# Split activations in slots at 256, 320 and 384 modulo 512 bytes, in place of one offset for all

## The chip, the core and the metric

The kernel runs on one core of a Trainium2 chip. The metric is the device time of one execution in microseconds (us).

## What is computed

Three stages follow each other, all on float32 numbers. `relu2` attention without a softmax comes first, then an MLP with a leaky relu, then an MLP with a squared relu:

```
B, S, D = 2, 3008, 256;  d_qk = 64;  d_ff = 2048
scores = (z @ z.T) / S;  attn = maximum(scores, 0) ** 2
x = u * (attn @ v)                                  # 6016 rows of 256
h = x @ w1_in;   x = maximum(0.01 * h, h) @ w1_out
h = x @ w2_in;   y = (s * maximum(h, 0) ** 2 + b) @ w2_out
```

## The kernel before

**Precision.** A float32 matrix product is made of three products in the type `float32r`. Every operand is split into a rounded part `hi` and the rest `lo`, and the kernel adds hi·hi, hi·lo and lo·hi in PSUM. Activations that are made on the way are split by `split_parts`, which hands out a pair of tiles `hi` and `lo`. Each is 128 partitions by 2 by 512 float32 numbers, so 4096 bytes in each partition. The pool `parts` keeps three slots for `hi` and three for `lo`, used in turn.

**Tiles.** There are 12 tiles of tokens. Ten have 512 columns and two have 448. A matmul's moving operand is a row of 512 or 448 columns, 2048 or 1792 bytes in a partition. Its weights are 128 columns, 512 bytes.

**Attention** (lines L351 and L425). It has 12 steps for each tile, 144 in all. A step makes the scores of two blocks of keys (six matmuls L351, weights `zk`, moving `zq`), then adds the values of an earlier step (24 matmuls L425, weights `stat_v`, moving `hi` and `lo`). These matmuls use 64 rows, and two of them, one for each half of the rows, run at once. So a step has 3 pairs of scores and 12 pairs of values. The square of the scores is split by `att_parts`.

**MLPs** (lines L500 and L519). The loop `for m, pr, q in quads` has 96 passes: 2 MLPs, 6 pairs of tiles, 8 blocks of d_ff. `product` (L500) makes the first layer from seven Strassen products of three matmuls each, with weights `stat_i` and moving operand `top`. `queue_second` (L519) makes the second layer with weights `stat_o` and moving operand `hi` and `lo` of the pass before. Each tile of a pass has 12 such matmuls. They are taken from a queue, eight after each third of the first-layer products. So in a pass 21 matmuls of L500 alternate with three runs of eight of L519, and a tile's twelve lie in two of these runs.

**Places in SBUF.** The pools lie one behind the other from the left (from low addresses), and `edge`, `z` and `c` from the right end. Worked out from the declarations and read from the built program, every SBUF operand of these matmuls begins, modulo 512 bytes in its partition, at 256 when it lies left, and at 448 when it lies right:

| operand | read by | before | after |
|---|---|---|---|
| weights `stat_v`, `stat_i`, `stat_o` | L425, L500, L519 | 256 | 256 |
| `hi`, `lo` | L425, L519 | 256 in all three slots | 256, 320, 384 by slot |
| `zk` (weights) and `zq` | L351 | 448 | 320 |
| `top` of B11 and T2, every second pair | L500 | 448 | 320 |
| all other `top` | L500 | 256 | 256 |

Parts within a tile lie multiples of 512 bytes apart, so the offset holds for each of them. B11 and T2 take their `top` from `cpool` on the right for every second pair of tiles. `tpool` on the left serves the others. There are four such pairs of 512 columns and two of 448 in the 12 pairs of both MLPs, with 8 passes each.

**Order.** [...] The program writes out each engine's list, and semaphores hold an instruction until its operands are there. `keep_busy` (L614) puts matmuls on a tile of zeros, which takes a `hi` slot, ahead of the first scores and again at step 2.

Of the kernel before, what the change touches and what calls it, by code (L numbers as in the profile page):

```python
# [10 lines left out]
F32 = mybir.dt.float32  # L11
F32R = mybir.dt.float32r
# [4 lines left out]
P = 128  # L17
# [3 lines left out]
QT = 512  # L21
# [7 lines left out]
def relu2_attention__then__leaky_mlp__then__relu2_mlp_kernel(  # L29
# [52 lines left out]
    parts = ctx.enter_context(tc.tile_pool(name="parts", bufs=3))  # L82
# [234 lines left out]
    def take(n):  # L317
        for _ in range(min(n, len(queue))):
            queue.popleft()()

    def split_parts(a, n):
        hi = parts.tile([P, 2, QT], F32R, tag="hi", name="hi")
        lo = parts.tile([P, 2, QT], F32R, tag="lo", name="lo")
        return [(y[:, :, :n]) for y in (hi, lo)]


# [16 lines left out]
    def scores(t, p):  # L343

        n = tiles[t][2]
        f = ps_f.tile([P, 2, QT], F32, tag="f", name="f")
        for i, (wh, xh) in enumerate(((0, 0), (1, 0), (0, 1))):
            for j in range(2):
                kb, rows = 2 * p + j, slice(j * DZ, (j + 1) * DZ)
                lhsT = zk[tiles[t][0], kb // 4][rows, wh, kb % 4 // 2, :]  # L350
                nc.tensor.matmul(f[:, j, :n], lhsT=lhsT, rhs=zq[t][rows, xh, :n], start=i == 0, stop=i == 2)  # L351
        return f[:, :, :n]
# [10 lines left out]
    def first_parts(f):  # L363

        a = work.tile([P, 2, QT], F32, tag="a", name="a")
        hi, lo = split_parts(a, QT)
        for j in range(2):
            nc.scalar.activation(out=a[:, j], in_=f[:, j], func=AF.Relu, scale=scale)
            nc.scalar.activation(out=a[:, j], in_=a[:, j], func=AF.Square)
            nc.vector.tensor_copy(out=hi[:, j], in_=a[:, j])  # L370
            nc.vector.tensor_sub(out=lo[:, j], in0=a[:, j], in1=hi[:, j].bitcast(F32))
        return hi, lo

    def att_parts(t, p, a):
        hi, lo = split_parts(a, tiles[t][2])
        (nc.scalar.copy if p % 2 and (t or p > 1) else nc.vector.tensor_copy)(out=hi, in_=a)  # L376
        nc.vector.tensor_sub(out=lo, in0=a, in1=hi.bitcast(F32))  # L377
        return hi, lo
# [195 lines left out]
    with tc.manual_schedule():  # L574
# [3 lines left out]
        raw_pool = lctx.enter_context(tc.tile_pool(name="raw", bufs=3))  # L578
        single = lctx.enter_context(tc.tile_pool(name="single", bufs=1))
        edge = ctx.enter_context(tc.tile_pool(name="edge", bufs=1, side="right"))  # L580
        edge.tile([P, 8], F32, tag="edge", name="edge")
        zpool = rctx.enter_context(tc.tile_pool(name="z", bufs=2, side="right"))
        ps_f = fctx.enter_context(tc.tile_pool(name="ps_f", bufs=2, space=bass.MemoryType.PSUM))
        tpool = cpool = ps_x = None
# [20 lines left out]
            if i:  # L605
                load_v(0, g, into=v_early.get(g))

        zeros = parts.tile([P, 2, QT], F32R, tag="hi", name="zeros")
        nc.vector.memset(zeros[:, 0].bitcast(F32), 0.0)  # L609
        idle = ps_a.tile([P, QT], F32, tag="acc", name="idle")  # L610

# [100 lines left out]
        for step in range(n_att):  # L712
# [6 lines left out]
            f = scores(t, p)  # L719
# [41 lines left out]
        def spread(ti):  # L761

            if not before:
                return
            m, pr, q, cs = before
            c = cs[ti]
            hi, lo = split_parts(c, tiles[pr[0]][2])
            (nc.scalar.copy if m == 1 else nc.vector.tensor_copy)(out=hi, in_=c)  # L768
            nc.vector.tensor_sub(out=lo, in0=c, in1=hi.bitcast(F32))  # L769
            queue_second(m, pr, q, ti, hi, lo)  # L770
# [9 lines left out]
        for m, pr, q in quads:  # L780
            n = tiles[pr[0]][2]
            k = pair_of.index((m, pr))
# [102 lines left out]
```

## Time and profile before

| | |
|---|---|
| median of two runs | 1460.42 us (1460.34 to 1460.51) |
| the profiled execution | 1460.41 us |
| its span, first to last instruction | 1458.6 us |
| outside the span | 1.8 us |
| PE (matmuls) busy | 1453.2 us, 100% |
| PEld (weight loads, beside PE) busy | 1211.4 us, 83% |
| DVE busy | 1113.1 us, 76% |
| ACT busy | 920.3 us, 63% |
| POOL busy | 91.6 us, 6% |

The profile is one execution. PE's busy time is from a matmul's start to its modelled end, and matmuls overlap, so a busy PE says only that some matmul is always under way. What a matmul costs is the time from its start to the start of the next. The attention runs until 474 us, the MLPs to the end.

### The profile page before, as it was taken

To read this page: it belongs to the slowest core of one execution; us is meant where nothing else is said; L and a number is where in the kernel's file an instruction comes from. 1 tells how busy PE (TensorE), PEld (TensorE's weight loads), DVE (VectorE), ACT (ScalarE), POOL (GpSimd) and SP (SyncE) were. 2 spreads that over 40 slices of the span, in tenths; PEclk is the share of its full clock that TensorE was granted. 3 is DMA by queue.
4 is the path that set the end of the run, shared out by engine and by line. 5 is a ranking of instruction groups with operands and counts; after the bars stand their busy time and mean duration, and the time that the engine had idled before them with its cause. 6 is when DMAs were issued, how large, how long until landed. Compare 5 with 4: busy or idle time off the path is not lost.

```text
span 1458.6 us, 20850 instructions
## 1 busy us (share of the span) xinstructions
PE 1453.2 (100%) x8584; PEld 1211.4 (83%) x8584; DVE 1113.1 (76%) x1461; ACT 920.3 (63%) x1143; POOL 91.6 (6%) x71
## 2 busy tenths in 40 slices
PE   9999999999999999999999999999999999999998
PEld 7888888888888788888889888888888888988887
DVE  7999978999986566666657666667878777787866
ACT  8888888988888455454555555554545455555544
POOL 1221200221214000000000000000000000000000
PEclk9999999999999999999999999999999999999999
DMA  5244333544545301000000103330010101010000
GB/s 177 80 161 160 142 121 112 163 149 163 181 168 200 143 0 58 1 26 29 23 36 15 41 0 124 143 139 28 19 40 1 55 1 58 1 54 1 22 8 29
DMA packets 40319, 112.03 MB, mean 77 GB/s; under 512 B 4128, under 2 KB 16544, under 8 KB 38176
## 3 DMA queue, kind: packets, MB, share of 16 engines
q1 hardware_dynamic: 39792, 110.31, 21.6%
q8 instruction: 67, 1.10, 0.3%
q10 hardware_dynamic: 368, 0.39, 0.1%
q14 instruction: 28, 0.23, 0.0%
q0 software_dynamic: 64, 0.00, 0.0%
HBM read 69.14 MB, written 41.55 MB: 76 GB/s over the span
## 4 chain that ended last, share of the span: by engine, by line
PE 100%; DVE 0%; ACT 0%; issue 0%
PE acc L519 35%; PE x L500 31%; PE acc L425 26%; PE f L351 7%; PE idle L614 0%; PE acc L446 0%; ACT y_half L548 0%; DVE x_sb L543 0%; DVE zeros L609 0%; PE f L566 0%; DVE ones L594 0%
## 5 line engine op out<-in xcount | busy, mean ns | idle before, releaser
L500 PE MATMUL x<-top,stat_i 128*128 128x512 f32 (+1 forms) x2016 | 499.1, 386 | 0.0
L519 PE MATMUL acc<-hi,stat_o 128*128 128x512 f32 (+1 forms) x1536 | 483.4, 386 | 0.0
L500 PEld LDWEIGHTS x<-top,stat_i 128*128 128x128 f32 x2016 | 377.6, 188 | 74.5 <-issue 1.2
L425 PE MATMUL acc<-hi,stat_v 64*128 64x512 f32 (+1 forms) x2256 | 366.2, 384 | 0.0
L519 PEld LDWEIGHTS acc<-hi,stat_o 128*128 128x128 f32 x1536 | 288.3, 188 | 55.5 <-issue 0.2
L519 PE MATMUL acc<-lo,stat_o 128*128 128x512 f32 (+1 forms) x768 | 296.2, 386 | 0.0
L769 DVE TENSOR_TENSOR lo<-c,hi 128x1024 fp32r<-128x1024 f32 (+1 forms) x192 | 230.6, 1201 | 38.3 <-ACT hi L768 35.1
L792 ACT COPY a<-x 128x512 f32<-128x512 f32 (+1 forms) x96 | 55.5, 578 | 319.7 <-PE x L500 319.2
L425 PEld LDWEIGHTS acc<-hi,stat_v 64*128 64x128 f32 x2256 | 211.6, 184 | 43.6 <-issue 1.1
L377 DVE TENSOR_TENSOR lo<-a,hi 128x1024 fp32r<-128x1024 f32 (+1 forms) x143 | 197.4, 1380 | 27.7 <-ACT hi L376 24.0
L425 PE MATMUL acc<-lo,stat_v 64*128 64x512 f32 (+1 forms) x1104 | 214.2, 385 | 0.0
L519 PEld LDWEIGHTS acc<-lo,stat_o 128*128 128x128 f32 x768 | 144.1, 188 | 27.4
L357 ACT ACTIVATE a<-f 128x1024 f32<-128x1024 f32 (+1 forms) x143 | 143.5, 1003 | 17.1 <-PE f L351 11.4
L359 ACT ACTIVATE a<-a 128x1024 f32<-128x1024 f32 (+1 forms) x143 | 149.4, 1045 | 4.2
L795 DVE TENSOR_TENSOR a<-x,a 128x512 f32<-128x512 f32 (+1 forms) x96 | 65.3, 680 | 84.5 <-PE x L500 83.5
L829 DVE TENSOR_TENSOR c<-x,a 128x512 f32<-128x512 f32 (+1 forms) x96 | 65.3, 680 | 77.0 <-PE x L500 77.0
L425 PEld LDWEIGHTS acc<-lo,stat_v 64*128 64x128 f32 x1104 | 103.4, 184 | 22.1 <-issue 0.7
L351 PE MATMUL f<-zq,zk 64*128 64x512 f32 (+1 forms) x864 | 121.7, 387 | 0.0
L759 ACT ACTIVATE c<-c 128x1024 f32<-128x1024 f32 (+1 forms) x96 | 100.2, 1044 | 3.0
L768 ACT CAST hi<-c 128x1024 fp32r<-128x1024 f32 (+1 forms) x96 | 98.7, 1028 | 1.5
L351 PEld LDWEIGHTS f<-zq,zk 64*128 64x128 f32 x864 | 81.3, 185 | 16.8 <-ACT zq L300 0.7
L818 DVE TENSOR_TENSOR c<-x,a 128x512 f32<-128x512 f32 (+1 forms) x96 | 65.1, 678 | 38.1 <-PE x L500 37.5
(84 smaller groups left out, 1072.2 us busy)
## 6 DMA issues: line engine op xcount, KB each, us to landing
in_d<-stage_i SPq DMA_DIRECT2D x16, 896.0 KB, 5.9
stat_i<-in_d SPq DMA_DIRECT2D x16, 896.0 KB, 4.6
x_in<-x_d SPq DMA_DIRECT2D x20, 512.0 KB, 4.2
raw_w<-in_w_in_dram SPq DMA_DIRECT2D x16, 512.0 KB, 4.0
raw_w<-in_w_out_dram SPq DMA_DIRECT2D x16, 512.0 KB, 3.9
out_d<-stage_o SPq DMA_DIRECT2D x8, 1024.0 KB, 6.6
stat_o<-out_d SPq DMA_DIRECT2D x8, 1024.0 KB, 6.5
u_sb<-in_uT_dram SPq DMA_DIRECT2D x10, 512.0 KB, 5.6
```

Of the source, the lines that this page charges most:

```text
L351: nc.tensor.matmul(f[:, j, :n], lhsT=lhsT, rhs=zq[t][rows, xh, :n], start=i == 0, stop=i == 2)
L357: nc.scalar.activation(out=a, in_=f, func=AF.Relu, scale=scale)
L359: nc.scalar.activation(out=a, in_=a, func=AF.Square)
L377: nc.vector.tensor_sub(out=lo, in0=a, in1=hi.bitcast(F32))
L425: nc.tensor.matmul(acc[:, :n], lhsT=w[rows, wh, o:o + P], rhs=x[rows, blk % 2, :n], start=blk == 0 and i == 0, stop=bool(closing and last),)
L500: nc.tensor.matmul(x[:, :n], lhsT=w[:, wh, left, :], rhs=r[:, xh, :n], start=first and i == 0, stop=i == 2, skip_group_check=not first,)
L519: nc.tensor.matmul(acc[dh][:, :n], lhsT=w[:, q % 2, wh, o:o + P], rhs=x[:, f, :n], start=q == 0 and f == 0 and i == 0, stop=last,)
L759: nc.scalar.activation(out=c, in_=c, func=AF.Square)
L768: (nc.scalar.copy if m == 1 else nc.vector.tensor_copy)(out=hi, in_=c)
L769: nc.vector.tensor_sub(out=lo, in0=c, in1=hi.bitcast(F32))
L795: nc.vector.tensor_tensor(out=u2, in0=x2, in1=s1, op=ALU.add)
L829: nc.vector.tensor_tensor(out=c21, in0=x2, in1=s1, op=ALU.add)
```

## The change

The three slots become three pairs of tiles with names of their own (`hi0`, `lo0`, `hi1`, ...), in the order hi0, lo0, a gap of 64 bytes, hi1, lo1, a gap of 64 bytes, hi2, lo2, and a gap of 384 bytes. The split with the number k takes slot k modulo 3. What follows in the left pools begins at 256 again. `edge` grows from 32 to 160 bytes, so that what lies on the right moves from 448 to 320. The tile of zeros lies in `hi0`.

```diff
+    GAPS = (0, 64, 64, 384)
+    for k, gap in enumerate(GAPS):
+        if gap:
+            parts.tile([P, gap // 4], F32, tag=f"gap{k}", name="gap", bufs=1)
+        if k < 3:
+            for name in ("hi", "lo"):
+                parts.tile([P, 2, QT], F32R, tag=f"{name}{k}", name=name, bufs=1)
+    places_of = iter(range(1 << 20))
+
     def split_parts(a, n):
-        hi = parts.tile([P, 2, QT], F32R, tag="hi", name="hi")
-        lo = parts.tile([P, 2, QT], F32R, tag="lo", name="lo")
+        k = next(places_of) % 3
+        hi = parts.tile([P, 2, QT], F32R, tag=f"hi{k}", name="hi", bufs=1)
+        lo = parts.tile([P, 2, QT], F32R, tag=f"lo{k}", name="lo", bufs=1)
         return [(y[:, :, :n]) for y in (hi, lo)]
...
-        edge.tile([P, 8], F32, tag="edge", name="edge")
+        edge.tile([P, 40], F32, tag="edge", name="edge")
...
-        zeros = parts.tile([P, 2, QT], F32R, tag="hi", name="zeros")
+        zeros = parts.tile([P, 2, QT], F32R, tag="hi0", name="zeros", bufs=1)
```

On every engine the instructions stand in the same order as before, ten lines further down in the file. What moves is one wait of DVE at the start of the program. Before, DVE's list from the first split on reads so (`hi` and `lo` are the split parts, `a` the squared scores, `stat_v` and `zk` parts of the weights):

```order
L370 CAST hi<-a 128x512 [waits Activation_49]
L371 TENSOR_TENSOR lo<-a,hi 128x512 [waits DVE_49]
L370 CAST hi<-a 128x512 [waits Activation_49]
L371 TENSOR_TENSOR lo<-a,hi 128x512 [waits DVE_49]
L637 CAST stat_v<-raw_v 128x256 [waits DMAHW2_49]
L638 TENSOR_TENSOR stat_v<-raw_v,stat_v 128x256 [waits DVE_49]
L376 CAST hi<-a 128x1024 [waits Activation_49]
L377 TENSOR_TENSOR lo<-a,hi 128x1024 [waits DVE_49]
L116 TENSOR_TENSOR stat_v<-raw_v,stat_v 128x768 [waits DMAHW6_49,Activation_49]
L292 CAST zk<-zr_early 128x256 [waits DMAHW7_49,DMAHW0_49]
L293 TENSOR_TENSOR zk<-zr_early,zk 128x256 [waits DVE_49]
L376 CAST hi<-a 128x1024 [waits PE_49,Activation_49]
```

And now, the same stretch of DVE's list:

```order
L380 CAST hi<-a 128x512 [waits PE_49,Activation_49]
L381 TENSOR_TENSOR lo<-a,hi 128x512 [waits DVE_49]
L380 CAST hi<-a 128x512 [waits Activation_49]
L381 TENSOR_TENSOR lo<-a,hi 128x512 [waits DVE_49]
L647 CAST stat_v<-raw_v 128x256 [waits DMAHW2_49]
L648 TENSOR_TENSOR stat_v<-raw_v,stat_v 128x256 [waits DVE_49]
L386 CAST hi<-a 128x1024 [waits Activation_49]
L387 TENSOR_TENSOR lo<-a,hi 128x1024 [waits DVE_49]
L116 TENSOR_TENSOR stat_v<-raw_v,stat_v 128x768 [waits DMAHW6_49,Activation_49]
L292 CAST zk<-zr_early 128x256 [waits DMAHW7_49,DMAHW0_49]
L293 TENSOR_TENSOR zk<-zr_early,zk 128x256 [waits DVE_49]
L386 CAST hi<-a 128x1024 [waits Activation_49]
```

The wait for PE has gone from the third split to the first. In both programs it is a wait for the same point of PE's list, the 24th matmul, which is the last of the five idle ones of step 2 that read the tile of zeros. The first split now overwrites that tile, where before the third did.

## Rows read from the trace of the kernel before

**Rows 1.** The page's first, second and fourth part: PE, its granted clock, the chain.

```profile
PE 1453.2 (100%) x8584; PEld 1211.4 (83%) x8584; DVE 1113.1 (76%) x1461; ACT 920.3 (63%) x1143; POOL 91.6 (6%) x71
...
PEclk9999999999999999999999999999999999999999
...
PE 100%; DVE 0%; ACT 0%; issue 0%
```

**Rows 2.** Groups by line and shape: count | busy us, mean ns | idle before.

```profile
L500 PE MATMUL x<-top,stat_i 128*128 128x512 f32 x1680 | 422.6, 390 | 0.0
L519 PE MATMUL acc<-hi,stat_o 128*128 128x512 f32 x1280 | 407.8, 389 | 0.0
...
L425 PE MATMUL acc<-hi,stat_v 64*128 64x512 f32 x1880 | 308.9, 387 | 0.0
...
L519 PE MATMUL acc<-lo,stat_o 128*128 128x512 f32 x640 | 249.3, 389 | 0.0
...
L425 PE MATMUL acc<-lo,stat_v 64*128 64x512 f32 x920 | 180.4, 389 | 0.0
...
L519 PE MATMUL acc<-hi,stat_o 128*128 128x448 f32 x256 | 76.3, 367 | 0.0
...
L519 PE MATMUL acc<-lo,stat_o 128*128 128x448 f32 x128 | 47.0, 367 | 0.0
```

**Rows 3.** PE in order of time, MLP, 512 columns: start us, us, matmuls.

```profile
580.24 1.56 PE L500 MATMUL x<-top,stat_i 128*128 128x512 f32 x6
...
581.64 0.85 PE L500 MATMUL x<-top,stat_i 128*128 128x512 f32 x3
...
583.25 0.39 PE L519 MATMUL acc<-lo,stat_o 128*128 128x512 f32 x1
...
584.15 1.52 PE L500 MATMUL x<-top,stat_i 128*128 128x512 f32 x6
...
590.50 2.02 PE L500 MATMUL x<-top,stat_i 128*128 128x512 f32 x8
```

**Rows 4.** PE in order of time, MLP, 448 columns.

```profile
756.02 1.40 PE L500 MATMUL x<-top,stat_i 128*128 128x448 f32 x6
...
761.81 1.37 PE L500 MATMUL x<-top,stat_i 128*128 128x448 f32 x6
...
763.02 0.78 PE L500 MATMUL x<-top,stat_i 128*128 128x448 f32 x3
```

**Rows 5.** PE in order of time, one attention step, 512 columns.

```profile
101.03 0.85 PE L351 MATMUL f<-zq,zk 64*128 64x512 f32 x6
101.72 0.39 PE L425 MATMUL acc<-hi,stat_v 64*128 64x512 f32 x2
...
103.33 0.39 PE L425 MATMUL acc<-lo,stat_v 64*128 64x512 f32 x2
...
104.46 0.85 PE L351 MATMUL f<-zq,zk 64*128 64x512 f32 x6
```

**Rows 6.** PE in order of time, one attention step, 448 columns.

```profile
230.27 0.77 PE L351 MATMUL f<-zq,zk 64*128 64x448 f32 x6
...
233.31 0.77 PE L351 MATMUL f<-zq,zk 64*128 64x448 f32 x6
```

**Rows 7.** DVE's subtractions by line: duration ns min/median/max.

```profile
L377 DVE TENSOR_TENSOR lo<-a,hi x143: 1084/1225/2360, 11.9 to 478.6; 128x1024 fp32r<-128x1024 f32 x119, 128x896 fp32r<-128x896 f32 x24
...
L769 DVE TENSOR_TENSOR lo<-c,hi x192: 1081/1224/1227, 491.2 to 1448.4; 128x1024 fp32r<-128x1024 f32 x160, 128x896 fp32r<-128x896 f32 x32
```

**Rows 8.** All engines in order of time, the first splits.

```profile
7.33 1.42 PE L614 MATMUL idle<-zeros 128*128 128x512 f32 x5
...
8.04 0.43 DVE L370 CAST hi<-a 128x512 fp32r<-128x512 f32 x1 [1.05 <-ACT a L369]
...
9.65 0.69 DVE L371 TENSOR_TENSOR lo<-a,hi 128x512 fp32r<-128x512 f32 x1
...
10.40 0.19 PEld L425 LDWEIGHTS acc<-lo,stat_v 64*128 64x128 f32 x2 [0.26 <-DVE lo L371]
```

## The prediction

> **What bounds the kernel now.** I read the page's totals and its chain first. PE is busy for 1453.2 us of the span of 1458.6 us, and the chain of work that ended last is PE's for 100% of its length [rows 1]. [...] The groups by line then show no idle time before PE's matmuls [rows 2]. PE thus paces the kernel, and what counts is the time from the start of one matmul to the start of the next. That is read from the view in order of time.
>
> There the same instruction does not always take the same time, and the offsets are what differs. In the MLP from 584.15 to 590.50 us, 28 matmuls of 512 columns, both operands at 256, take 6.35 us, or 226.8 ns each [rows 3]. The six from 580.24 to 581.64 us are B11 and T2 of a pair whose `top` lies at 448, with weights at 256. They take 1.40 us, 233.3 ns each [rows 3]. Engines, waits and shapes are the same. After them the moving offset is back at 256, but the next seven matmuls, to 583.25 us, still take 1.61 us, 230.0 ns each, before 226.8 returns [rows 3]. I call that settling: 0.023 us after each such group. With 448 columns the order is reversed. 28 matmuls at equal offsets, from 756.02 to 761.81 us, take 5.79 us, 206.8 ns each, and the six at 448 over 256, from 761.81 to 763.02 us, take 201.7 ns [rows 4]. So the distance between the offset of the moving operand and that of the weights costs up to 6.5 ns in a matmul, in either direction.
>
> In the attention the scores have both operands at 448 and the values both at 256, so that the distance changes where one follows the other. The three pairs of scores take 0.69 us, 230 ns each, and the seven pairs of values behind them 1.61 us, again 230 ns. The last five are at 226 ns [rows 5]. A step takes 3.43 us, where 15 pairs at 226.8 ns would be 3.40 us, so 0.03 us of it is settling. A step of 448 columns takes 3.04 us, 202.7 ns a pair, and doesn't settle at 206.8 at all [rows 6].
>
> **The change part by part.** It removes and adds no instruction. It gives two thirds of all splits a distance of 64 or 128 bytes from the weights, moves scores and some `top` from 448 to 320, and moves one wait of DVE.
>
> *How many.* Matmuls of 512 columns on `hi` and `lo`: 1280 and 640 in the MLPs, and 1880 and 920 in the attention, which run two at once, so 1400 pairs [rows 2]. That is 3320 steps of PE, a third of them, 1107, in each slot. Of 448 columns the MLPs have 256 and 128, so 128 in each slot [rows 2]. The attention's of 448 are left as they are, since they don't keep to either level now.
>
> *The price of 64 and of 128* is not in the trace. The measured distances are 0 and 192, at 226.8 and 233.3 ns. The bounds are one such step of 6.5 ns to either side of 226.8, since the 448-column rows show that a distance can also gain. I take each at the row that it is nearest to: 64 as 0, 128 as 192.
>
> - Slot 2, at 128: 1107 by 6.5 ns is +7.2 us. Its 448-column matmuls save 128 by 5.1 ns, -0.7 us.
> - Slot 1, at 64: 0, with bounds of -7.2 and +7.2 us.
> - Settling in the MLPs: a pass has two tiles with two runs each. The 80 passes of 512 columns have 320 runs, of which 107 lie in slot 2. At 0.023 us, +2.5 us.
> - `top` at 320 in place of 448, so 64 and taken as 0: four pairs by 8 passes by 6 matmuls are 192 by -6.5 ns, -1.2 us. Two pairs of 448 columns are 96 by +5.1 ns, +0.5 us. 32 settlings fall away, -0.7 us. Together -1.4 us.
> - Scores at 320: in slots 0 and 1 they now stand within 64 of the values, so the settling of 0.03 us falls away in two thirds of the 120 steps of 512 columns, -2.4 us. If it stays, 0.
> - The wait: the first split (8.04 us) now waits for the five idle matmuls, which end at 7.33 + 1.42 = 8.75 us [rows 8], so it starts 0.7 us later. Behind it on DVE stand its subtraction, the second split and its subtraction, almost back to back, the last of which ends at 10.34 us. PE waits for that one already, 0.26 us at 10.40 us [rows 8]. So nothing hides it there: +0.7 us, at least 0 if the lists make it up. The third split loses the wait, which was over long before.
> - DVE and ACT: no cost. The subtraction with operands at 448 and 256 (L769) has a median of 1224 ns, and that with both at 256 (L377) one of 1225 ns [rows 7]. Their durations don't follow the offset, and PE doesn't wait for them but at the start.
>
> The sum is 7.2 - 0.7 + 0 + 2.5 - 1.4 - 2.4 + 0.7 = **+5.9 us**. The profiled execution took 1460.41 us, the median is 1460.42, so they need no correction: **1466.3 us**.
>
> [...]
>
> **The rivals.**
>
> A, the forecast: nearest rows, 1466 us.
>
> B, both new distances are a step cheaper. For it speaks that distance gains 5.1 ns at 448 columns [rows 4]. Against it: in the long run no stretch of 512 columns stands under 226 ns. 2213 matmuls by -6.5 ns are -14.4 us. `top` gains 13 ns on 192, -2.5 us, and 0.7 us of settling. All 120 steps lose their settling, -3.6 us. With the wait, -20.5 us: 1440 us.
>
> C, slower: both distances cost what 192 does, and three offsets in turn keep PE from ever settling. Its place is the runs of L519 and the whole attention step. 2213 by 6.5 ns is +14.4 us, 213 runs by 0.023 us +4.9 us, and five more pairs in each step at 230 in place of 226.8 ns +1.9 us. 256 matmuls of 448 columns save 1.3 us. With the wait, +20.6 us: 1481 us. It decides from the point at which 64 costs what 192 does. For it: one change of distance is enough to unsettle seven matmuls [rows 3]. Against it: 64 is nearer to 0.
>
> D, the change doesn't do what it says: something else than distance makes the 6.5 ns (that `top` lies in another pool, say), and only the wait is left, 1461 us. Against it: a few microseconds later the same line runs at 226.8 ns from the left pool, in both widths with opposite signs [rows 3, 4]. [...]
>
> **How the numbers follow.** A 0.40, B 0.25, C 0.20, D 0.15. A's own range, by slot 1 and the settling in the attention, is 1457 to 1474 us. For 8 in 10 I go from 1444 us, which leaves out the part of B that reaches its full price (0.12), to 1478 us, which leaves out the end of C (0.08). About 2% of the time, 29 us, is what a measurement of this kernel can tell from no change. Under 1431 us needs more than B's full price, over 1490 us a distance that costs some 13 ns on all 2213 matmuls. I give each 0.03 and leave 0.94 for no change.
>
> **What would show it.** The view in order of time, by slot: runs of L519 on slot 0 near 227 ns, on slot 1 the same, on slot 2 near 233, and B11 and T2 of every second pair at 227. In the attention, steps of slots 0 and 1 at 3.40 us. At the start, the first split at about 8.75 us and PE's wait of 10.40 us about 0.7 us later. If slot 1 stands near 220 or 233 ns, the price of 64 is wrong and B or C is right. If all slots stand at 226.8, D is. What would upset the whole sum is that a matmul's time depends on the offsets of its neighbours in more ways than one distance, so that no slot has a price of its own.

## The result, and the profile after

The changed kernel took 1474.37 us (1473.31 and 1475.43 in two runs) against 1460.42 us before. The ratio is 1.0093, with a 95% interval of 1.0073 to 1.0114. It is thus about 0.9% slower: the interval lies clear of 1, but inside the 2% that counts as no change here. The profiled execution took 1473.31 us with a span of 1471.5 us, 12.9 us longer than the 1458.6 us of before. Lines of the changed kernel stand ten lower in its file from the first edit on: L351, L425, L500 and L519 are now L361, L435, L510 and L529.

The page of the changed kernel (busy times, granted clock, the chain by engine) answers to [rows 1]:

```profile
PE 1465.4 (100%) x8584; PEld 1213.0 (82%) x8584; DVE 1112.8 (76%) x1461; ACT 921.3 (63%) x1143; POOL 91.6 (6%) x71
...
PEclk9999999999999999999999999999999999999999
...
PE 99%; DVE 0%; DMA 0%; ACT 0%; issue 0%; DVEq 0%
```

PE has the same 8584 instructions at the same granted clock (0.999 and 1.000 on average), and grew from 1453.2 to 1465.4 us of busy time. DVE and ACT moved by 1 us at most. So the loss lies in PE's own pace and in no other engine.

The groups by line and shape (count | busy us, mean ns | idle before) answer to [rows 2]:

```profile
L510 PE MATMUL x<-top,stat_i 128*128 128x512 f32 x1680 | 425.4, 392 | 0.0
L529 PE MATMUL acc<-hi,stat_o 128*128 128x512 f32 x1280 | 412.6, 393 | 0.0
L435 PE MATMUL acc<-hi,stat_v 64*128 64x512 f32 x1880 | 311.8, 391 | 0.0
```

Their mean durations rose by 2 to 4 ns, without idle time. Since matmuls overlap (those of 512 columns in the table below last 387 to 393 ns on average and start 227 to 234 ns apart), I summed the time from each start to the next over the whole trace of either kernel, by line and width. Two matmuls on 64 rows that start together (3 ns apart at the median in both traces) count once, and the very last matmul, which has no next, is left out:

| line of before, columns | matmuls | before, us | after, us | difference |
|---|---|---|---|---|
| L351 scores, 512 | 360 | 84.3 | 84.0 | -0.3 |
| L425 values, with L446, 512 | 1410 | 322.7 | 327.5 | +4.8 |
| L500 `top` products, 512 | 1680 | 384.3 | 387.0 | +2.7 |
| L519 split products, 512 | 1920 | 435.8 | 443.2 | +7.4 |
| L500, 448 | 336 | 68.7 | 68.2 | -0.5 |
| L519, 448 | 384 | 79.0 | 77.8 | -1.2 |

The rest of PE's work is unchanged to 0.1 us, and the sum is +12.9 us, the difference of the spans.

PE in order of time, MLP, 512 columns, answers to [rows 3]:

```profile
600.08 1.53 PE L510 MATMUL x<-top,stat_i 128*128 128x512 f32 x6
601.45 0.63 PE L529 MATMUL acc<-hi,stat_o 128*128 128x512 f32 x2
...
603.30 1.53 PE L510 MATMUL x<-top,stat_i 128*128 128x512 f32 x6
...
611.88 0.62 PE L529 MATMUL acc<-hi,stat_o 128*128 128x512 f32 x2
...
615.06 0.39 PE L529 MATMUL acc<-lo,stat_o 128*128 128x512 f32 x1
...
622.66 0.62 PE L529 MATMUL acc<-hi,stat_o 128*128 128x512 f32 x2
...
624.52 1.54 PE L510 MATMUL x<-top,stat_i 128*128 128x512 f32 x6
```

The allocation tells which slot each piece reads. From 601.45 to 603.30 us eight split products read slot 1 (320) and take 1.85 us, 231 ns each. The six `top` products ahead of them, at 256, take 1.37 us, 228 ns each, though both their operands lie at 256. From 611.88 to 615.06 us everything is at 256, and 14 products take 3.18 us, 227 ns each. From 622.66 to 624.52 us eight products read slot 2 (384) and take 1.86 us, 232.5 ns each. Over the trace the means of L519 are 228.6 ns in slot 0, 231.7 in slot 1 and 232.5 in slot 2, against 227.1 before.

The scores of five attention steps in a row answer to [rows 5]:

```profile
102.51 0.86 PE L361 MATMUL f<-zq,zk 64*128 64x512 f32 x6
...
105.94 0.85 PE L361 MATMUL f<-zq,zk 64*128 64x512 f32 x6
...
109.43 0.85 PE L361 MATMUL f<-zq,zk 64*128 64x512 f32 x6
...
112.91 0.86 PE L361 MATMUL f<-zq,zk 64*128 64x512 f32 x6
...
116.35 0.85 PE L361 MATMUL f<-zq,zk 64*128 64x512 f32 x6
```

From one start to the next is a step. In slots 0, 1, 2 and 0 again they take 3.43, 3.49, 3.48 and 3.44 us, where the steps took 3.43 us before [rows 5].

The start, all engines in order of time, answers to [rows 8]:

```profile
7.23 1.41 PE L624 MATMUL idle<-zeros 128*128 128x512 f32 x5
...
8.75 0.43 DVE L380 CAST hi<-a 128x512 fp32r<-128x512 f32 x1 [1.64 <-PE idle L624]
...
11.02 0.18 PEld L435 LDWEIGHTS acc<-lo,stat_v 64*128 64x128 f32 x2 [0.53 <-DVE lo L381]
...
12.99 0.86 PE L361 MATMUL f<-zq,zk 64*128 64x512 f32 x6
```

In the trace of before, the scores that now start at 12.99 us started here:

```profile
12.33 0.85 PE L351 MATMUL f<-zq,zk 64*128 64x512 f32 x6
```

The first cast waits for the idle products, as foreseen, and PE is 0.66 us later behind it.

### The profile page after: what moved, and what is told of

It is laid out like the page before. It is cut to its first block, busy times and chain, and to the rows that moved or that the text cites. A ratio compares the mean times of both kernels' runs of the same rounds, so it can differ in the third digit from the quotient of the medians.

```text
span 1471.5 us, 20850 instructions
## 1 busy us (share of the span) xinstructions
PE 1465.4 (100%) x8584; PEld 1213.0 (82%) x8584; DVE 1112.8 (76%) x1461; ACT 921.3 (63%) x1143; POOL 91.6 (6%) x71
## 4 chain that ended last, share of the span: by engine, by line
PE 99%; DVE 0%; DMA 0%; ACT 0%; issue 0%; DVEq 0%
PE acc L529 35%; PE x L510 31%; PE acc L435 26%; PE f L361 7%; DMA zr<-in_zT_dram 0%; PE acc L456 0%; DVE lo L381 0%; PE idle L624 0%; DVE zq L301 0%; DVE zk L634 0%; DVE hi L380 0%; ACT y_half L558 0%; DVE x_sb L553 0%; PE f L576 0%; DVE zk L632 0%
## 5 line engine op out<-in xcount | busy, mean ns | idle before, releaser
L510 PE MATMUL x<-top,stat_i 128*128 128x512 f32 (+1 forms) x2016 | 501.5, 388 | 0.0
L529 PE MATMUL acc<-hi,stat_o 128*128 128x512 f32 (+1 forms) x1536 | 487.5, 388 | 0.0
L510 PEld LDWEIGHTS x<-top,stat_i 128*128 128x128 f32 x2016 | 377.7, 188 | 77.6 <-issue 1.2
L435 PE MATMUL acc<-hi,stat_v 64*128 64x512 f32 (+1 forms) x2256 | 369.0, 386 | 0.0
L529 PEld LDWEIGHTS acc<-hi,stat_o 128*128 128x128 f32 x1536 | 288.5, 188 | 58.4 <-issue 0.2
L529 PE MATMUL acc<-lo,stat_o 128*128 128x512 f32 (+1 forms) x768 | 298.1, 388 | 0.0
L435 PEld LDWEIGHTS acc<-hi,stat_v 64*128 64x128 f32 x2256 | 212.3, 185 | 45.1 <-issue 1.1
L435 PE MATMUL acc<-lo,stat_v 64*128 64x512 f32 (+1 forms) x1104 | 215.7, 388 | 0.3 <-DVE lo L381 0.2
L529 PEld LDWEIGHTS acc<-lo,stat_o 128*128 128x128 f32 x768 | 144.3, 188 | 29.4
L435 PEld LDWEIGHTS acc<-lo,stat_v 64*128 64x128 f32 x1104 | 103.8, 185 | 22.9 <-DVE lo L381 1.1
L361 PE MATMUL f<-zq,zk 64*128 64x512 f32 (+1 forms) x864 | 121.1, 385 | 0.4 <-DVE zq L301 0.4
L361 PEld LDWEIGHTS f<-zq,zk 64*128 64x128 f32 x864 | 81.1, 184 | 17.8 <-DVE zq L301 0.8
```

The costliest lines, as they stand in the source:

```text
L435: nc.tensor.matmul(acc[:, :n], lhsT=w[rows, wh, o:o + P], rhs=x[rows, blk % 2, :n], start=blk == 0 and i == 0, stop=bool(closing and last),)
L510: nc.tensor.matmul(x[:, :n], lhsT=w[:, wh, left, :], rhs=r[:, xh, :n], start=first and i == 0, stop=i == 2, skip_group_check=not first,)
L529: nc.tensor.matmul(acc[dh][:, :n], lhsT=w[:, q % 2, wh, o:o + P], rhs=x[:, f, :n], start=q == 0 and f == 0 and i == 0, stop=last,)
```

## The experiments

**The halves of the change.** The first kernel moves only the right-hand pools, the second only the slots (the change without its edit of `edge`, which stays at 8). The edit of the first:

```diff
-        edge.tile([P, 8], F32, tag="edge", name="edge")
+        edge.tile([P, 40], F32, tag="edge", name="edge")
```

> The kernel before with one half of the change: the right-hand pools at 320 modulo 512, the split activations' slots all at 256 as they were. Distance theory (each 64-byte distance between the two operands of a matmul has a price of its own: from the changed kernel's intervals about 231 ns at 64, 232.5 at 128, 233.3 at 192 against 226.7 at 0 for 512 columns, 201 to 203 against 206.7 for 448): the scores and the early top products go from distance 192 to 64, 360 x -0.9 ns, 192 x -2.7 ns, together about -1 us: 1459.5 us (1457 to 1461). Change theory (a constant distance is free, only going from one distance to another costs some 24 ns over six matmuls): just as many changes as before, 1460.4. Right-pool theory (the loss comes from the right-hand pools): the whole +13.9, 1474.

> The other half alone: slots at 256, 320 and 384, the right-hand pools back at 448. Distance theory: the split products of the MLP and the values as in the changed kernel, that is +7.4 - 1.2 + 4.8, and the share of the third line's intervals that settles after a change, about +3: 1474 us (1471 to 1477). Change theory: the same size, since the slots alternate just as often. Right-pool theory: only the wait at the start, 1461.

Measured: the right-hand pools alone 1461.21 us, ratio 1.0004 (0.9995 to 1.0013); the slots alone 1472.74 us, 1.0083 (1.0069 to 1.0096). The loss lies with the slots. One thing in my first expectation was careless: scores have queries and keys both in right-hand pools, so their own distance was 0 before and after, and the -0.9 ns on them had no ground.

**One distance throughout.** The next kernels give every moving operand, split halves, `top` and queries, the same distance from its weights, which all stay at 256. At distance 0 the edge alone does it:

```diff
-        edge.tile([P, 8], F32, tag="edge", name="edge")
+        edge.tile([P, 56], F32, tag="edge", name="edge")
```

For distance d a gap of d bytes goes ahead of the slots and of the queries, and the edge is sized to match; here d = 64:

```diff
+        if not zq:
+            zpool.tile([P, 16], F32, tag="zgap", name="zgap", bufs=1)
         m = zpool.tile([P, 2, QT], F32R, tag="zq", name="zq", bufs=2)
...
+    parts.tile([P, 16], F32, tag="gap", name="gap", bufs=1)
...
-        edge.tile([P, 8], F32, tag="edge", name="edge")
+        edge.tile([P, 40], F32, tag="edge", name="edge")
```

> From the kernel before: every moving operand (split halves, early top products, scores) and its weights at the same place, 256 modulo 512; nothing ever changes its distance. Distance theory: scores 360 x about -5 ns, values 1410 x -1.9, early top 192 x -7, their neighbours 1488 x -1.4, against 168 products of 448 columns at +5: together -7, 1453.5 us (1450 to 1458). Change theory: the same -7. A theory by which offsets do nothing: 1460.4.

> From the kernel before: every moving operand 64 bytes above its weights modulo 512, all through; nothing ever changes its distance. This tells two theories apart. Distance theory: 5,370 products of 512 columns at +4.3 ns and 1,074 of 448 columns at -5.7 ns against the run with distance 0, +17: about 1470 us (1465 to 1476). Change theory: as the run with distance 0, 1453.5 (1450 to 1458).

> Every moving operand 128 bytes above its weights modulo 512, all through. Graded theory (the level rises with the distance): slot 2 of the changed kernel took 0.8 ns more than slot 1, 5,370 x 0.8 over the run with distance 64: 1467.5 us (1465 to 1471). Theory of one step (any distance but 0 costs the same once it is constant): 1463.1 (1461 to 1465).

> Every moving operand 192 bytes above its weights, all through. Graded theory: the early top products of the kernel before (448 over 256) took 233.3 to 233.7 ns; 5,370 x 6.7 over distance 0, less 1,074 products of 448 columns x 2: 1489 us (1480 to 1490). Theory of one step: 1463.1 (1461 to 1465), and then 233.3 is the cost of the change, not of the distance.

> Every moving operand 256 bytes from its weights modulo 512. The level theory holds by now for 0, 64, 128 and 192 (1454.8, 1463.1, 1485.0 and 1487.8 us); open is its shape, and so where one should put operands that can't lie together. Mirror theory (only the shorter way round 512 counts): the top of the curve, 1489 us (1486 to 1494). Theory of 256 (the distance counts modulo 256): as distance 0, 1454.8 (1453 to 1457). One-way theory (rises all the way to 512): 1490 (1487 to 1496).

> Distance 320. Mirror theory: as 192, 1488 us (1485 to 1491). Theory of 256: as 64, 1463 (1461 to 1466). One-way theory: above 192, 1492 (1489 to 1500).

> Distance 384. Mirror theory: as 128, 1485 us (1482 to 1488). Theory of 256: as 128 as well, 1485. One-way theory: 1495 (1490 to 1510).

> Distance 448, the moving operand 64 bytes below its weights. Mirror theory: as 64, 1463 us (1461 to 1466). Theory of 256: as 192, 1488 (1485 to 1491). One-way theory: the dearest of all, 1500 (1490 to 1520).

Measured, with the mean from start to start of L519's products in the MLP:

| distance | us | ratio to before (95%) | 512 columns, ns | 448 columns, ns |
|---|---|---|---|---|
| 0 | 1454.80 | 0.9964 (0.9951 to 0.9978) | 226.9 | 202.6 |
| 64 | 1463.08 | 1.0017 (1.0008 to 1.0025) | 229.4 | 200.1 |
| 128 | 1485.01 | 1.0169 (1.0155 to 1.0183) | 232.4 | 203.6 |
| 192 | 1487.84 | 1.0184 (1.0170 to 1.0198) | 233.4 | 202.3 |
| 256 | 1454.37 | 0.9961 (0.9946 to 0.9976) | 226.9 | 202.5 |
| 320 | 1462.10 | 1.0013 (1.0004 to 1.0022) | 229.0 | 200.1 |
| 384 | 1484.47 | 1.0161 (1.0146 to 1.0176) | 232.4 | 203.5 |
| 448 | 1487.02 | 1.0182 (1.0165 to 1.0199) | 233.4 | 202.3 |

PE in order of time in five of these kernels. Each pair of rows holds the same 14 products of 512 columns, six of `top` and eight of L519 (here L519 or L523), and the second row starts the next ones. Distance 0:

```profile
613.02 1.52 PE L500 MATMUL x<-top,stat_i 128*128 128x512 f32 x6
...
616.19 1.52 PE L500 MATMUL x<-top,stat_i 128*128 128x512 f32 x6
```

Distance 64:

```profile
605.08 1.54 PE L504 MATMUL x<-top,stat_i 128*128 128x512 f32 x6
...
608.29 1.53 PE L504 MATMUL x<-top,stat_i 128*128 128x512 f32 x6
```

Distance 128:

```profile
613.41 1.56 PE L504 MATMUL x<-top,stat_i 128*128 128x512 f32 x6
...
616.66 1.56 PE L504 MATMUL x<-top,stat_i 128*128 128x512 f32 x6
```

Distance 192:

```profile
604.13 1.56 PE L504 MATMUL x<-top,stat_i 128*128 128x512 f32 x6
...
607.40 1.56 PE L504 MATMUL x<-top,stat_i 128*128 128x512 f32 x6
```

Distance 256:

```profile
612.56 1.52 PE L504 MATMUL x<-top,stat_i 128*128 128x512 f32 x6
...
615.74 1.52 PE L504 MATMUL x<-top,stat_i 128*128 128x512 f32 x6
```

They take 3.17, 3.21, 3.25, 3.27 and 3.18 us. What follows: a constant distance has a level of its own. At 512 columns the level rises from 0 to 192 and starts again at 256, with 0.4 ns at most between two distances that lie 256 apart, so in these runs the distance counts modulo 256; the mirror and the one-way theory both fall with the run at 256. The theory that only a change of distance costs fell with the run at 64, 8.3 us above that at 0, and the theory of one step with the run at 128, 21.9 us above that at 64. The sizes that I had foretold for 64 and 128 were both missed, 1470 us (1465 to 1476) against 1463.08 and 1467.5 us (1465 to 1471) against 1485.01. They came from intervals of the changed kernel, where offsets alternate. The kernels at 0 and 256 beat both the kernel before and the changed one.

**Levels and changes.** From the changed kernel, this one puts the split slots at 320 and everything else at 256. It also starts with slot 1, so that the first split does not overwrite the zeros:

```diff
+    GAPS = (64, 0, 0, 448)
...
-    places_of = iter(range(1 << 20))
+    places_of = iter(range(1, 1 << 20))
...
-        edge.tile([P, 8], F32, tag="edge", name="edge")
+        edge.tile([P, 56], F32, tag="edge", name="edge")
```

> As the run with distance 0, but all three slots of the split activations at 320: split products 64 bytes above their weights, the top products of the MLP and the scores at distance 0. The same share of products lies at distance 0 or 64 as nowhere else, and in the MLP they alternate in pieces of six, so the distance changes every six products. Level theory (a constant distance of 64 costs 2.4 ns for 512 columns, as the run with distance 64 shows, and nothing else): 1,920 split products of the MLP x 2.4 and 1,410 values x 2.0, less 666 products of 448 columns x 2.5, +5.8 on 1454.8: 1460.6 us (1458 to 1463). Level and change theory (each change of distance costs as well): as in slot 1 of the changed kernel, 1,920 x 4.8, 1,680 top products x 2.5, 1,410 values x 3, less 1.0: +17, 1472 us (1468 to 1476). It would then be slower than the run with distance 64 everywhere.

Measured: 1470.84 us (1470.15 to 1472.44), ratio 1.0070 (1.0057 to 1.0083). It has fewer products at distance 64 than the kernel that has nothing else, and yet is 7.8 us slower. Its MLP in order of time:

```profile
609.68 1.53 PE L510 MATMUL x<-top,stat_i 128*128 128x512 f32 x6
611.05 0.63 PE L529 MATMUL acc<-hi,stat_o 128*128 128x512 f32 x2
...
612.90 1.53 PE L510 MATMUL x<-top,stat_i 128*128 128x512 f32 x6
```

Six `top` products at distance 0 take 1.37 us, 228 ns each, and eight split products at 64 take 1.85 us, 231 ns each, the same figures as in the changed kernel around slot 1. Both are above their levels, 226.9 and 229.4 ns. So the changes of distance cost as well.

**The wait at the start.** The changed kernel with the first split in slot 1, away from the zeros of the idle products. Every later split moves on by one slot too:

```diff
-    places_of = iter(range(1 << 20))
+    places_of = iter(range(1, 1 << 20))
```

> The changed kernel with the first split activations in slot 1, so that slot 0 is left to the zeros of the idle products and the first cast waits for none of them. Level and change theory: only the wait goes, 0.3 to 0.7 us faster than the changed kernel: 1473.8 us (1472.5 to 1475). Wait theory (the wait at the start holds up more than it shows): back towards 1461.

Measured: 1472.52 us (1472.29 to 1473.03), ratio 1.0080 (1.0066 to 1.0094). Its span is 1470.8 us against 1471.5, 0.7 us less. Its interval overlaps that of the changed kernel, and its time stays far from 1461, so the wait is a small part at most.

## Why the prediction was right, and where its sizes were off

The prediction was 1466 us in a range of 1444 to 1478, with 0.94 on no change; the time is 1474.4. The loss of 13.9 us is more than twice the forecast 5.9 us, and the time lies at the upper end of A's own range of 1457 to 1474. The stated range holds it because it was drawn wide for the rivals, and not because the sum was right.

That the offset of the moving operand against the weights sets PE's pace is shown by the eight kernels above. Between 0 and 192 they differ by 33 us with the same instructions, and L519's products of 512 columns by 6.5 ns. Rival D is out.

That it is the distance of the two, and not the offset of the moving operand alone, the eight kernels do not show, since the weights lie at 256 in all of them. Two rows of before speak for the distance: `top` at 448 over weights at 256 takes 233.3 ns [rows 3], and scores at 448 over weights at 448 take 230 ns [rows 5]. But these scores are three pairs between two changes of offset, and weights alone were not moved in any kernel. What in the chip makes the offsets count stays open too.

The terms, with what the trace of the changed kernel gives by the same count of products (in us, from the means by slot against the mean of all slots before). Without the last row, which is part of the one above it, the measured terms add up to +12.9:

| term | predicted | measured |
|---|---|---|
| slot 2, 512 columns | +7.2 | MLP 647 x 5.4 ns = +3.5, values 480 x 4.1 ns = +2.0 |
| slot 1, 512 columns | 0 | MLP 648 x 4.6 ns = +3.0, values 480 x 4.0 ns = +1.9 |
| 448 columns of the MLPs' split products | -0.7 | -1.2 |
| settling in the MLPs | +2.5 | slot 0 +0.9, `top` at 256 1488 x 2.2 ns = +3.2 |
| `top` in the right-hand pools and at 448 columns | -1.4 | -0.5 and -0.5 |
| scores at 320, settling in the attention | -2.4 | scores -0.3, values of slot 0 +0.9 with most of the wait in them |
| the wait | +0.7 | +0.66, at 12.99 us, in the row above |

**Slot 1 is the step that was mis-sized.** I took 64 as 0 because it is nearer, with bounds of 7.2 us to either side; it cost 4.9 us. Of the MLP's 3.0 us about half is the level: at a constant 64 the products take 229.4 ns, 2.5 above distance 0, and 648 x 2.5 ns = 1.6 us. The rest goes with the changes of distance, as in the kernel with only the slots at 64.

The attention's 1.9 us has another source. Between these two rows of the changed kernel, 11 pairs of values in slot 1 take 2.57 us, 234 ns each, and do not come down:

```profile
106.63 0.40 PE L435 MATMUL acc<-hi,stat_v 64*128 64x512 f32 x2
...
109.20 0.39 PE L435 MATMUL acc<-hi,stat_v 64*128 64x512 f32 x2
```

In the kernel with the slots alone, whose scores lie at 448 and not at 320, the same 11 pairs take 2.52 us, 229 ns each:

```profile
108.86 0.39 PE L435 MATMUL acc<-hi,stat_v 64*128 64x512 f32 x2
...
111.38 0.39 PE L435 MATMUL acc<-hi,stat_v 64*128 64x512 f32 x2
```

The distances are equal in both kernels, 0 for scores and 64 for values. Over the whole trace the values of slot 1 take 111.8 us in the first and 109.9 us in the second, against 109.8 us before. So this part of the loss comes from the slots and the moved right-hand pools together, and values at 64 can run at two paces. The prediction had named this as what would upset its sum: a matmul's time depends on its neighbours' offsets, so that in the attention slot 1 has no price of its own. In the MLPs the means of slots 1 and 2 differ by 0.3 ns at most between the two kernels.

**Slot 2 at the price of 192** was nearly right: the level of 128 is 232.4 ns and that of 192 is 233.4. In the MLPs slot 2 stands at its level, 232.5 ns, with no more on top. 1.7 us of the term are missing, mostly in the values, whose mean of 228.9 ns before already held some settling: with distance 0 throughout it is 227.3 ns.

**Settling in the MLPs** was counted behind the runs of slot 2 alone, 107 of them. But six `top` products at 256 alternate with about eight of the split ones, so in slots 1 and 2 the distance changes at every seam. `top` products that the change doesn't touch rose from 228.1 to 230.3 ns, +3.2 us in all: 1.8 us of it stands behind products of slot 2, and 1.2 us behind those of slot 1, where the prediction had nothing. The kernel with only the slots at 64 shows this apart from the levels.

**Settling in the attention** was to fall away with the scores within 64 of the values. It did not: steps of slot 0 take 3.44 us, those of slot 1 3.49. The prediction also misnamed what changes there. Scores at 448 over 448 and values at 256 over 256 both have distance 0, so at their seam no distance changes, only the offset of both operands. In the kernel with distance 0 throughout the scores are 3.40 us apart, which is the figure I had foretold for slots 0 and 1:

```profile
100.77 0.84 PE L351 MATMUL f<-zq,zk 64*128 64x512 f32 x6
...
104.17 0.84 PE L351 MATMUL f<-zq,zk 64*128 64x512 f32 x6
```

So the settling of 0.03 us was real, and lying 64 apart is not enough to remove it.

Rival B fell with the run at distance 64, which is dearer and not cheaper at 512 columns. Rival C held in the attention, where slot 1 runs near the 233 ns of 192, but was too dear for slot 1 in the MLPs at 231.7 ns. That PE would never settle did not hold: the 14 products from 611.88 us take 227 ns each. The time lies between A and C.

## What to carry to other kernels

Where PE paces a kernel, read the time from start to start of one kind of matmul and sort it by the address of its operands; the profile's groups show the loss only as a few ns in a mean. Give moving operands and weights the same offset in every pool that feeds one stretch of PE, above all where products of two pools alternate: here that took 0.36% (ratio 0.9964, 0.9951 to 0.9978) off a kernel whose other engines all had slack (PEld, the busiest of them, was busy for 83% of the span [rows 1]). Moving operands 256 bytes from their weights throughout did as well (0.9961); 0 and 256 in turn were not tried. When a change spreads buffers over several offsets, count the seams between products, those of untouched operands too, and not the buffers.

## What was not expected of the hardware

Distance 0 does not have one pace at 448 columns. Before, 28 products took 206.8 ns each [rows 4]. In the kernel with distance 0 throughout, 14 of the same products, from the first row to the second, take 2.84 us, 202.9 ns each:

```profile
756.13 1.38 PE L500 MATMUL x<-top,stat_i 128*128 128x448 f32 x6
...
758.97 1.99 PE L500 MATMUL x<-top,stat_i 128*128 128x448 f32 x9
```

So part of the 5.1 ns that I took for a gain of distance was a pace into which PE had fallen; at 64 the products take 200.1 ns. What decides between the two paces stays open.

A matmul's own distance is not the whole story either. With only the right-hand pools moved, scores have both operands at 320 and values both at 256, so every product of the attention has distance 0, but steps take 3.45 us in place of 3.40:

```profile
99.85 0.86 PE L351 MATMUL f<-zq,zk 64*128 64x512 f32 x6
...
103.30 0.86 PE L351 MATMUL f<-zq,zk 64*128 64x512 f32 x6
```

Weights are loaded beside running matmuls (PEld is busy for 83% of the span next to PE's 100% [rows 1]), at the seams too. In the trace of before, weights of scores, at 448, are loaded from 12.11 us on, beside values at 256 that start at 12.10 us and last 0.39 us:

```profile
12.10 0.39 PE L425 MATMUL acc<-hi,stat_v 64*128 64x512 f32 x2
12.11 0.64 PEld L351 LDWEIGHTS f<-zq,zk 64*128 64x128 f32 x6
```

Whether it is such a load at one offset beside a matmul at the other that costs, or the jump of the moving operand itself, no run shows; in all kernels with one distance the weights lay at 256, so these two don't come apart there.
